# First group of a fused attention and FFN kernel: the leftover queries' product in front of the next k v

## The chip, the cores and the metric

One core of one Trainium2 chip. The metric is the device time of one execution in microseconds; the numbers below are medians of several runs. The engines are called PE (TensorE matmul; PEld are its weight loads), ACT (ScalarE), DVE (VectorE), POOL (GpSimd) and SP (SyncE, which issues most DMAs).

## What is computed

An attention block without softmax, its root-mean-square norm, and a feed-forward block with a product of two gates; all in float32:

```python
kv = np.einsum('bhsd,bhse->bhde', k, v)          # B, H, S, D = 8, 8, 576, 64
out = np.einsum('bhsd,bhde->bhse', q, kv)
rms = np.sqrt(np.mean(out * out, axis=-1, keepdims=True) + 1e-06)
x = (out / rms * g_norm)                          # to (B*S, H*D) = (4608, 512)
a = x @ w1                                        # 512 x 1024
b = x @ w2
h = a * b @ w3                                    # 1024 x 1024
return h @ w_out                                  # 1024 x 512
```

The kernel multiplies w3 by w_out first, and g_norm into w1 and w2.

## The kernel before

**Tiles and groups.** Each batch has 576 tokens. 512 of them form one group of the feed-forward part, and the 64 left over of all eight batches form a ninth group. So the loop at the end of the kernel runs over nine groups of 512 tokens. A group goes through four gate steps (p = 0 to 3, function `gates`, L896) and a projection (`project`, L1129, for group 0; `project_twice` for the others). Both use a Strassen-Winograd scheme (`winograd`, L724): seven products of half the size in each dimension, in place of eight. In the first group a gate product is 8 records of L738 in the profile (a float32 matmul leaves two records), a projection product 16. The seven products are p1 (a11 b11), p5 (s1 t1), u2 (s2 t2), then s4 b22, u3 (s3 t3), a12 b21 and a22 t4. Later groups apply the scheme twice and have other lines (L1030, L1288).

**Attention beside it.** While group T is multiplied, the attention of batch T + 1 is worked off in small pieces. `steps(b)` (L591) lists the pieces of batch b in eight steps, and `winograd` calls `between()` at two places, after u2 and in front of a22 t4; each call takes the next step. In group 0 the gate p = 0 takes none, so steps 0 and 1 stand in gate 1, 2 and 3 in gate 2, 4 and 5 in gate 3, and 6 in the projection after u2, 7 in front of its a22 t4. A step runs first its "ends" (what was begun in the step before and has to be finished), then its "fs".

**The pieces that matter.**
- `kv(g, beside)`, called by `begin_kv` (L497): k transposed times v for four heads, 36 matmuls of 64 x 64 (72 records of L350), then six small copies on ACT (L358, L360) into `kv_sb`. Its two result banks come from the pool `ps_at`, unless `beside` gives two banks: then it takes their last 64 columns. `begin_kv` afterwards has SP load the next k and v.
- `product(h)`, called by `finish(h)`: q times kv for half of the heads, 64 records of L428, into one bank of `ps_mm` and one of `ps_at` in batch 1; then `norm`.
- `product_left` (L438), for odd batches: the 64 leftover queries of this batch and of the one before, 32 records of L447, into two banks of `ps_at` (their first 256 columns). It reads `qT_left`, the transposed queries. For the odd batches 3 and 5 it has the k v of the next batch put into the same banks (L454, L455).
- `norm` (L388 on): squares on ACT (L395), sums on DVE (L396), a square root on ACT (L400), then reciprocal and multiplication on DVE (L402, L405). It is a generator with three parts; its first `next` issues squares and sums.
- Transposes through the DMA, `turn_by_dma`: a copy that puts the halves of the words apart (L309, L311), a transposing DMA on SP (L313), and a copy back (L323). In batch 1 the queries, `qT_left` and the first half of x have these copies on ACT, the second half of x and the leftover x on POOL. `qT_left` is begun in step 3 and finished among the ends of step 5, behind the ends of the first half of x in the list, and on ACT behind gate 3's copy u3.

**Order.** On PE, POOL and SP the instructions run in the order in which the program issues them. On ACT and DVE, in group 0, the compiler's planner orders them by readiness and by its own estimates of their cost; `tc.issue_after(x)` draws an edge that keeps instructions on x's engine behind x. A wait between two engines is put in wherever one uses the other's data.

**PSUM.** Eight banks: five in `ps_mm`, which the gate and projection products use, and three in `ps_at`, for attention.

Around the change, batch 1 before: step 5 issues the k v of batch 2 (first half), then the second q kv product of batch 1 with its norm. Step 6 issues the leftover product with its whole norm, and begins the transposes of the second half of x on POOL. Step 7 begins the transposes of the leftover x and of the next queries.

Of the kernel before, what the change touches and what calls it, by code (L numbers as in the profile page):

```python
# [22 lines left out]
def kernel(  # L23
# [36 lines left out]
    B, H, S, D = q.shape  # L60
# [4 lines left out]
    FIRST_OF_TWO = 2  # L65
# [18 lines left out]
    def bank(pool, tag):  # L84
        return pool.tile([P, 512], FP32, name=tag, tag=tag)

    loaded, copies, adds = {}, {}, {}
# [181 lines left out]
    def all_of(steps):  # L269
        for _ in steps:  # L270
            pass
# [61 lines left out]
    def attention(b):  # L333
# [55 lines left out]
        def norm(o_ps, dsts):  # L389

            n, w = len(o_ps), o_ps[0].shape[1]
            inv = work.tile([P, n, w // D], FP32, name="inv")
            for i in range(n):
                sq = work.tile([P, G], FP32, name=f"sq{0 if b > FIRST_OF_TWO else i}", bufs=1)[:, 0:w]
                nc.scalar.activation(sq, o_ps[i], AF.Square)  # L395
                adds["norm"] = nc.vector.tensor_reduce(  # L396
                    out=inv[:, i], in_=sq.rearrange("p (h d) -> p h d", d=D), axis=AX.X, op=ALU.add
                )
            yield
            nc.scalar.activation(inv, inv, AF.Sqrt, scale=1.0 / D, bias=eps_col)  # L400
            yield
            nc.vector.reciprocal(inv, inv)  # L402
            for i in range(n):
                m, k = dsts[i].shape[1:3]
                nc.vector.tensor_tensor(  # L405
                    out=dsts[i],
                    in0=o_ps[i].rearrange("p (m k d) -> p m k d", k=k, d=D),
                    in1=inv[:, i].rearrange("p (m k) -> p m k", k=k).unsqueeze(3).to_broadcast(
                        [P, m, k, D]
                    ),  # L410
                    op=ALU.mult,
                )
# [25 lines left out]
        def product_left():  # L438

            xn = st["left"] = work.tile([P, NP, 2, D], FP32, name="xn_left", bufs=1)  # L440

            o_ps = [bank(ps_at, "at") for _ in range(2)]
            for r in range(NP):
                for l in range(2):
                    for e in range(2):
                        rows = slice(e * D, (e + 1) * D)
                        nc.tensor.matmul(  # L447
                            o_ps[e][l * L:(l + 1) * L, r * D:(r + 1) * D],
                            lhsT=st["qT"][rows, r, l * L:(l + 1) * L],
                            rhs=kv_sb[(b - 1 + l) % 3][rows, r % 2 ^ e, e, r // 2, :],  # L450
                            start=True,
                            stop=True,
                        )
            if FIRST_OF_TWO < b < B - 1:  # L454
                batch(b + 1).begin_kv(0, o_ps)  # L455
            o_ps = [t[:, 0:NP * D] for t in o_ps]
            all_of(norm(o_ps, [xn[:, :, e:e + 1, :] for e in range(2)]))

        def turn(r):

# [58 lines left out]
        def finish(h):  # L519
            all_of(product(h))  # L520

        return SimpleNamespace(**{f.__name__: f for f in (
            start, begin_kv, begin_q, product, finish, turn, product_left,
            q_two_by_dma, q_by_dma, q_left_by_dma, x_by_dma, x_part_by_dma, x_left_by_dma, load_q_ahead,
        )})
# [3 lines left out]
    def batch(b):  # L529
        if b not in batches:  # L530
            batches[b] = attention(b)
        return batches[b]
# [58 lines left out]
    def steps(b):  # L591

        a = batch(b)
        a.start()
        more = b + 1 < B
        fs, ends = ([[] for _ in range(8)] for _ in range(2))

        def turn(i, f, *args, next_group=False):

            t = []

            def begin():
                t.append(f(*args))
                next(t[0])
                next(t[0])

            fs[i].append((begin,))  # L610
            (to_end if next_group else ends[i + 1]).append((lambda: all_of(t[0]),))

        if to_end:

            ends[0] += [(lambda: nc.gpsimd.tensor_copy(tick, late["p5"][:, 0, 0:1]),), *to_end]
        to_end.clear()
        odd = b % 2
        by_scalar, in_two = b >= FIRST_OF_TWO, b > FIRST_OF_TWO
        if b == 1:
            early.extend(a.q_two_by_dma(r) for r in (0, 1))  # L620
            q_first = list(early)
            fs[0].append((a.begin_kv, 0))

            def end_first():
                for t in q_first:
                    with tc.issue_after(copies["u3"][-1].ins):
                        next(t)
                    all_of(t)

            ends[1].append((end_first,))  # L630
        def begin_first():
            rest = a.product(0)
            next(rest)
            slots.setdefault(("p1", "p1"), []).insert(0, (all_of, rest))

        fs[2 if b == 1 else 1] += [
            (a.begin_kv, 1), (begin_first,) if by_scalar and not in_two else (a.finish, 0),
        ]
        if b == 1:
            last = {}  # L640

            def begin(name, behind, f, *args):
                last[name] = f(*args)
                with tc.issue_after(copies[behind][-1].ins):
                    next(last[name])
                next(last[name])

            def end(name, behind):
                with tc.issue_after(copies[behind][-1].ins):
                    next(last[name], None)  # L650
                all_of(last[name])

            fs[3] += [(begin, f"q{r}", "u3", a.q_two_by_dma, r) for r in (2, 3)]
            fs[3].append((begin, "left", "u3", a.q_left_by_dma))
            fs[4].append((begin, "x", "p1", a.x_by_dma, 0, nc.scalar.copy))
            ends[4] += [(end, "q2", "p1"), (end, "q3", "p5")]
            ends[5] += [(end, "x", "u2"), (end, "left", "u3")]
        elif by_scalar:
            turns_by_scalar(b)
        else:  # L660
            turn(1, a.q_two_by_dma, 2, 3)
            turn(2, a.x_by_dma, 0)
            if odd:
                turn(1, a.q_left_by_dma)
        second = 5 if b == 1 else 4
        if more:
            if not (in_two and odd):
                fs[second].append((batch(b + 1).begin_kv, 0))
        fs[second].append((a.finish, 1))
        if odd:  # L670
            fs[3 if in_two else second + 1].append((a.product_left,))
        if b == 1:
            turn(6, a.x_by_dma, 1)
            turn(7, a.x_left_by_dma, next_group=True)
        else:
            if not by_scalar:
                turn(5, a.x_by_dma, 1)
            if odd:
                turn(5, a.x_left_by_dma, next_group=more)
        if more and not by_scalar:  # L680
            turn(7 if b == 1 else 5, batch(b + 1).q_two_by_dma, 0, 1, next_group=True)
        if more:
            fs[7 if odd else 0].append((load_q_left, b + 1))
        return iter([lambda s=e + f: [f(*args) for f, *args in s] for e, f in zip(ends, fs)])
# [815 lines left out]

    for n, T in enumerate(groups):
        pieces = steps(T + 1) if n + 2 < NG else iter([])

        def prepare_some(pieces):
# [41 lines left out]
        for p in range(NF):  # L1546
# [22 lines left out]
            if T == 0:  # L1569
# [29 lines left out]
                if p + 1 == NF:  # L1599
                    allocate_projection()  # L1600
                    first, *others = zip(*(f(i) for i in range(NF) for f in (sum_ab, combine_w3o)))
                    with tc.issue_after(adds["c21"][p - 2].ins):
                        all_of(step() for step in first)
                    with tc.issue_after(adds["c12"][p - 1].ins):
                        all_of(step() for steps in others for step in steps)
# [57 lines left out]
```

## Time and profile before

| | |
|---|---|
| median of 3 runs | 743.08 us (742.86 to 744.15) |
| the profiled execution | 742.95 us, its span 741.0 us |
| granted clock of TensorE | 1.000 |
| PE idle from 82 us on, to the span's end | 3.4 us of 659.0 |
| small stretch of step 5 (k v, second q kv product) | 132.06 to 134.20 us |
| leftover product (step 6) | 146.49 to 147.11 us |

The span is the time from the first to the last instruction of one profiled execution. A timeline line gives start, duration, engine, line, operation, tiles, shape and count; what stands in brackets is the idle time before, with what ended it. Matmul durations overlap, since PE works on several at a time: distances between starts tell the pace. The chain of waits follows the work that ended last back from the end; where it names PE line after line, PE itself is what everything waits for. A record's "<-issue" means that the engine waited for nothing that the profile shows.

### The profile page before, as it was taken

The numbers are of one execution on the slowest core, as the hardware profiler recorded it, in microseconds if no ns is written. First come the engines' busy times: TensorE is split into PE (matmuls) and PEld (weight loads), VectorE is DVE, ScalarE is ACT, GpSimd is POOL, SyncE is SP. The second block draws the span as 40 slices with busy tenths as digits, with TensorE's granted clock in tenths as the row PEclk, the third lists the DMA queues.
The fourth block names the chain that finished last, engine by engine and source line by source line (L and its number), as shares of the span: only waits on it lengthen the run. The fifth ranks groups of instructions, "written<-read, shape, count | busy, mean of one in ns | idle before, by whom it ended". The sixth has DMA issues, their size and how long they took to land.

```text
span 741.0 us, 16817 instructions
## 1 busy us (share of the span) xinstructions
PE 735.2 (99%) x6839; PEld 658.3 (89%) x6839; DVE 622.0 (84%) x1237; ACT 379.0 (51%) x654; POOL 21.9 (3%) x29
## 2 busy tenths in 40 slices
PE   8999999999999999999999999999999999999998
PEld 6455788888899999999999999999999999999997
DVE  6877898967969689968996899689969987997797
ACT  6787777415552675257526752576177313212321
POOL 0000000131000000000000001000001000000000
PEclk9999999999999999999999999999999999999999
DMA  9997834599999698869986998588847762565454
GB/s 308 371 335 215 242 107 132 125 336 297 301 301 320 170 277 262 260 169 290 258 264 159 293 264 264 179 284 236 271 101 220 227 206 87 182 215 158 135 199 135
DMA packets 135456, 169.65 MB, mean 229 GB/s; under 512 B 78036, under 2 KB 110804, under 8 KB 135380
## 3 DMA queue, kind: packets, MB, share of 16 engines
q1 hardware_dynamic: 132928, 154.16, 69.0%
q10 hardware_dynamic: 2452, 14.42, 5.7%
q8 instruction: 54, 0.88, 0.5%
q14 instruction: 22, 0.18, 0.1%
HBM read 130.55 MB, written 20.71 MB: 204 GB/s over the span
## 4 chain that ended last, share of the span: by engine, by line
PE 97%; DMA 2%; ACT 0%; SPq 0%; issue 0%; DVE 0%; ACTq 0%
PE mm L738 38%; PE mm L1288 23%; PE mm L1030 21%; PE mm L708 7%; PE at L350 3%; PE at L738 2%; DMA raw<-in_moe_w_out_dram 2%; PE mm L428 1%; PE at L428 1%; PE at L695 1%; PE at L1331 0%; PE at L447 0%; PE at L370 0%; SPq L210 0%; ACT ab L162 0%; PE at L464 0%
## 5 line engine op out<-in xcount | busy, mean ns | idle before, releaser
L1079 ACT COPY slots<-mm 128x512 f32<-128x512 f32 x88 | 51.7, 587 | 126.3 <-PE mm L1288 83.3
L738 PE MATMUL mm<-xT,w_sb 128*128 128x256 f32 x448 | 102.9, 379 | 0.0
L738 PEld LDWEIGHTS mm<-xT,w_sb 128*128 128x128 f32 x448 | 84.4, 190 | 11.5 <-issue 0.5
L738 PE MATMUL mm<-xc,ws 128*128 128x256 f32 x336 | 76.1, 379 | 0.0
L738 PEld LDWEIGHTS mm<-xc,ws 128*128 128x128 f32 x336 | 63.8, 190 | 8.7
L756 ACT COPY slots<-mm 128x512 f32<-128x512 f32 x59 | 34.6, 587 | 68.9 <-PE mm L738 63.8
L708 PE MATMUL mm<-chunks,ab 128*128 128x512 f32 x128 | 60.7, 605 | 1.0 <-ACT chunks L163 0.8
L1083 DVE TENSOR_TENSOR slots<-mm,slots 128x512 f32<-128x512 f32 x66 | 45.1, 684 | 17.0 <-PE mm L1030 16.9
L1080 ACT COPY slots<-mm 128x384 f32<-128x384 f32 x88 | 42.4, 482 | 25.7 <-PE mm L1288 23.0
L1030 PE MATMUL mm<-ws,w3o_sb 128*128 128x128 f32 x350 | 53.9, 275 | 0.0
L396 DVE TENSOR_REDUCE inv<-sq 128x8 f32<-128x512 f32 (+1 forms) x40 | 24.6, 629 | 30.3 <-ACT sq L395 30.2
L1288 PE MATMUL mm<-w3o_sb,ab 128*128 128x128 f32 x368 | 48.9, 276 | 0.0
L1030 PEld LDWEIGHTS mm<-ws,w3o_sb 128*128 128x128 f32 x350 | 46.4, 192 | 0.0
L1288 PEld LDWEIGHTS mm<-w3o_sb,ab 128*128 128x128 f32 x368 | 45.4, 192 | 0.6
L1288 PE MATMUL mm<-w3o_sb,raw 128*128 128x128 f32 x340 | 43.5, 275 | 0.0
L708 PEld LDWEIGHTS mm<-chunks,ab 128*128 128x128 f32 x128 | 21.6, 190 | 23.4 <-issue 14.4
L1288 PEld LDWEIGHTS mm<-w3o_sb,raw 128*128 128x128 f32 x340 | 40.7, 192 | 0.0
L738 PE MATMUL mm<-xc,w_sb 128*128 128x256 f32 x160 | 38.5, 384 | 0.0
L1084 DVE TENSOR_TENSOR slots<-mm,slots 128x384 f32<-128x384 f32 x66 | 36.3, 551 | 2.3 <-PE mm L1288 1.9
L738 PE MATMUL mm<-xT,ws 128*128 128x256 f32 x160 | 38.1, 381 | 0.0
L323 ACT COPY xT<-xn 128x1024 uint16<-128x1024 uint16 x28 | 32.5, 1166 | 3.5 <-DMA xn<-xT 3.5
L738 PEld LDWEIGHTS mm<-xT,ws 128*128 128x128 f32 x160 | 30.1, 190 | 4.3 <-ACT slots L756 0.2
(243 smaller groups left out, 1639.8 us busy)
## 6 DMA issues: line engine op xcount, KB each, us to landing
w3o_sb<-w_l SPq DMA_DIRECT2D x21, 896.0 KB, 4.9
w3o_sb<-w3o_l SPq DMA_DIRECT2D x18, 896.0 KB, 6.6
raw<-in_moe_w_dram SPq DMA_DIRECT2D x31, 512.0 KB, 7.8
raw<-w3o_l SPq DMA_DIRECT2D x15, 896.0 KB, 4.7
w3o_sb<-w3o_l ACTq DMA_DIRECT2D x14, 896.0 KB, 4.5
k_sb<-in_k_dram SPq DMA_DIRECT2D x16, 576.0 KB, 4.9
v_sb<-in_v_dram SPq DMA_DIRECT2D x16, 576.0 KB, 6.4
q_sb<-in_q_dram SPq DMA_DIRECT2D x32, 256.0 KB, 3.9
```

The lines of the kernel that those rows point to most:

```text
L323: copy(words(dst), src)
L350: nc.tensor.matmul(ps[r * D:(r + 1) * D, :], lhsT=k_sb[rows, r, cols], rhs=v_sb[rows, r, cols], start=(j == 0), stop=(j == JS - 1),)
L396: adds["norm"] = nc.vector.tensor_reduce(out=inv[:, i], in_=sq.rearrange("p (h d) -> p h d", d=D), axis=AX.X, op=ALU.add)
L708: nc.tensor.matmul(sums_ps[half][m], lhsT=w3T[half, c][:, m, :], rhs=chunks[:, c, 1, :], start=(c == 0), stop=(c == KF - 1),)
L738: nc.tensor.matmul(ps[:, u, :], lhsT=lhsT(a_name, u, c), rhs=rhs(b_name, c),  start=(u == 0 and c == 0 and new), stop=(c == chunks - 1), s ...
L756: copies.setdefault(name, []).append(nc.scalar.copy(t, ps))
L1030: nc.tensor.matmul(ps[place // 4][:, place % 4, :], lhsT=x, rhs=y, start=new and place // 4 not in seen, stop=True, skip_group_check=True,)
L1079: nc.scalar.copy(z[:, 0:4], ps[0])
L1080: return nc.scalar.copy(z[:, 4:7], ps[1][:, 0:3])
L1083: nc.vector.tensor_add(z[:, 0:4], ps[0], z[:, 0:4])
L1084: nc.vector.tensor_add(z[:, 4:7], ps[1][:, 0:3], z[:, 4:7])
L1288: nc.tensor.matmul(ps[place // 4][:, place % 4, :], lhsT=x[:, c, :], rhs=y[:, c, :], start=new and place // 4 not in seen, stop=(c == 1), ...
```

## The change

For batch 1 only, three things. The leftover product is called in step 5 in place of the k v of batch 2, and has that k v put into its own two banks, right behind itself, as batches 3 and 5 do. The second q kv product follows, as before. The norm of the leftover product is no longer issued with it: `product_left` returns the generator, and step 6, where the leftover product was, runs the norm, with its first part behind the projection's copy u2 on ACT. The conditions for the other batches are written in another way and give the same calls.

```diff
-            if FIRST_OF_TWO < b < B - 1:
+            if b == 1 or FIRST_OF_TWO < b < B - 1:
                 batch(b + 1).begin_kv(0, o_ps)
             o_ps = [t[:, 0:NP * D] for t in o_ps]
-            all_of(norm(o_ps, [xn[:, :, e:e + 1, :] for e in range(2)]))
+            rest = norm(o_ps, [xn[:, :, e:e + 1, :] for e in range(2)])
+            if b > 1:
+                all_of(rest)
+            return rest
...
         second = 5 if b == 1 else 4
         if more:
-            if not (in_two and odd):
+            if not odd:
                 fs[second].append((batch(b + 1).begin_kv, 0))
+        if b == 1:
+            rest = []
+
+            def end_left():
+                with tc.issue_after(copies["u2"][-1].ins):
+                    next(rest[0])
+                all_of(rest[0])
+
+            fs[second].append((lambda: rest.append(a.product_left()),))
+            fs[second + 1].append((end_left,))
         fs[second].append((a.finish, 1))
-        if odd:
-            fs[3 if in_two else second + 1].append((a.product_left,))
+        if in_two and odd:
+            fs[3].append((a.product_left,))
```

## The prediction

> **What bounds the kernel now.** I read the page first, then the chain of waits, then the windows, then the timeline around the two places that the change touches. The page, its busy times and its chain by engine:
>
> ```profile
> PE 735.2 (99%) x6839; PEld 658.3 (89%) x6839; DVE 622.0 (84%) x1237; ACT 379.0 (51%) x654; POOL 21.9 (3%) x29
> ...
> PE 97%; DMA 2%; ACT 0%; SPq 0%; issue 0%; DVE 0%; ACTq 0%
> ```
>
> The windows view (stretch, length, then busy time and instructions of PE, PEld, DVE, ACT, POOL, then clock, DMA share, GB/s):
>
> ```profile
> 82.00:741.00 659.00, 655.64 (x6303) 614.40 (x6301) 558.44 (x1140) 317.44 (x561) 21.19 (x23) 1.00 0.73 219
> ```
>
> The reader is to see that TensorE sets the end, at full granted clock (1.00). From 82 us on, where the first group's gates begin, PE is idle for only 659.00 - 655.64 = 3.4 us, the tail after its last product included, and the wait table of PE has no entry at all in that stretch. So a stretch taken out of PE's row after 82 us comes off the end nearly in full, and no change here can win more than those 3.4 us by removing waits. What is left to win is time in which PE counts as busy but does not go at its best pace: at the switch between full 128x128 products and the small 64x64 ones.
>
> **The price of a switch.** The chain of waits gives stretches of PE with their lengths (start, us, what):
>
> ```profile
> 99.00 1.21 PE at L350 x72
> 100.21 12.29 PE mm L738 x56
> ...
> 146.56 0.62 PE at L447 x32
> 147.18 24.37 PE mm L738 x112
> ...
> 275.74 12.09 PE mm L738 x56
> ```
>
> 56 records of L738 that follow other full products take 12.09 us (last line), 0.2159 us each. The same 56 behind a k v take 12.29: 0.20 more. The 112 records behind the leftover product take 24.37, against 112 x 0.2159 = 24.18: 0.19 more. So every return from small to full products costs about 0.19 us, beside the small stretch itself. A leftover product that stands alone therefore costs 0.62 + 0.19 = 0.81 us of PE, as at 146.49:
>
> ```profile
> 143.80 2.75 PE L738 MATMUL mm<-raw 128*128 128x256 f32 x12
> 146.49 0.69 PE L447 MATMUL at<-kv_sb,qT_left 64*64 64x64 f32 x32
> 147.11 3.07 PE L738 MATMUL mm<-w3o_sb,raw 128*128 128x256 f32 x13
> ```
>
> Group 3 already has the order that the change gives the first group: leftover product, then k v in the same banks.
>
> ```profile
> 259.84 0.69 PE L447 MATMUL at<-kv_sb,qT_left 64*64 64x64 f32 x32
> 260.35 1.23 PE L350 MATMUL at<-v_sb,k_sb 64*64 64x64 f32 x72
> 261.51 0.71 PE L1030 MATMUL mm<-xc,w_sb 128*128 128x128 f32 x4
> ```
>
> From the first leftover matmul to the next full product it is 261.51 - 259.84 = 1.67 us. A k v alone is 1.21 (chain, first line above). So in front of a k v the leftover product adds 0.46 us, and its return to full products is paid already by the k v.
>
> **The change, part by part.**
>
> *PE, taken away* in the projection: 0.62 + 0.19 = 0.81. *PE, added* in gate 3: 0.46, because the stretch leftover, k v, second q kv product ends in the same return as now (at 134.20). Sum: -0.35 us. From the other side: if no return were saved and only the 1.21 + 0.62 - 1.67 = 0.16 between the starts counted, it would be -0.16. I take -0.35, since the two group-3 rows and the two return costs measure just this; -0.16 stays an end of the range.
>
> *A wait that is added.* The leftover product now stands first at 132.06 and reads qT_left, which ACT finishes just there:
>
> ```profile
> 130.44 0.59 ACT L756 COPY slots<-mm 128x512 f32<-128x512 f32 x1 [1.32 <-PE mm L738]
> 130.92 1.17 ACT L323 COPY qT_left<-ql_sb 128x1024 uint16<-128x1024 uint16 x1
> 134.41 2.23 ACT L323 COPY xT<-xn 128x1024 uint16<-128x1024 uint16 x2 [2.33 <-DMA xn<-xT]
> 136.56 0.20 ACT L358 COPY kv_sb<-at 128x64 f32<-128x64 f32 x1
> ```
>
> and the weight load that opens the small stretch today:
>
> ```profile
> 132.06 1.14 PEld L350 LDWEIGHTS at<-v_sb,k_sb 64*64 64x64 f32 x72 [0.33 <-issue]
> ```
>
> The copy ends at 130.92 + 1.17 = 132.09. How fast PE takes up an ACT copy the trace shows at 126.05 to 126.63: the weight load that waited for it begins at 126.68, 0.05 later. So the first leftover weight load can begin at 132.14 instead of 132.06: 0.08 us lost. Ends: nothing, if the copy is a little earlier; and 0.08 + 0.33 = 0.41, if the 0.33 that the weight loads stand idle at a switch (the line above) is only counted off after the wait. I take 0.08, since the small weight loads do not start before the full product is through anyway. Behind the waiting instruction on PE queue the k v, the second q kv product and gate 3's last product; nobody else waits for those closely: the k v's copies on ACT begin only at 136.56, behind the two xT copies.
>
> *PE in between.* From 132.14 to 147 everything on PE is 0.54 us later (0.46 + 0.08), then 0.27 earlier than now. The evictions and sums shift with it. What could be late: gate 3's c21, the projection's first products, the norm of product 1 (142.1) and the POOL copies behind it (142.17). The projection's combined x is first needed at 162.76 by L738 and its subtractions on DVE end at 159.5; the x copies on POOL end at 151.2 and DVE reads them at 154.39. Cover of 3 us each, so nothing. If that cover were gone, the loss would be at most the same 0.54.
>
> *SP, POOL, DMAs.* The k v's two loads (k and v of batch 2, second half) go out behind its reads, at 133.43 and 133.84 now, so some 0.5 later; they are first used at 171.48. The transposes of x on SP (144.54) and the POOL copies move by the same 0.5. No queue is passed by anything: the order on SP and POOL is as before. Price nothing.
>
> *PSUM.* The leftover product and the k v share two banks of ps_at, the second q kv product takes the third: three, as now. Two banks stay occupied until the leftover norm ends (149.13 + 0.76 = 149.9), and the next that asks for one is the k v at 171.48. Price nothing. The Trainium skill speaks against sharing here: "PSUM — Partial Sum Buffer", section "PSUM bank collisions raise a hardware error", says that two engines may not touch one bank in the same partitions at the same time, whatever the columns, so that such pairs get put one behind the other. By that rule ACT's k v copies and the leftover norm's readers would exclude each other; a k v copy lasts 0.2 to 0.43 us in this trace, so the rule would price a real clash at under 0.5. In the rows nothing clashes: the k v copies run from 136.56 to 137.85, the leftover's squares at 147.29.
>
> *The norm's end.* Its squares stay behind the projection's u2 copy (146.59) on ACT, by an explicit edge now. They no longer wait for PE. Its result is used by POOL at 151.17. Nothing.
>
> **Sum:** -0.35 + 0.08 = -0.27 us, between -0.35 + 0 = -0.35 and -0.16 + 0.41 = +0.25. The profiled execution took 742.95 (span 741.0 and 1.95 around it); with the change 742.68. The median of the three runs is 743.08, 0.13 above, so I forecast 743.08 - 0.27 = 742.8. That is 0.04%; under 0.2% (1.5 us) a measurement of this kernel can hardly tell a change from none.
>
> **Rivals.**
>
> 1. *The new wait eats the saving* (742.9 to 743.3). For it: copy and PE meet within 0.03 us, by chance. Against it: it can cost 0.41 at most, so it decides nothing at 0.2%. Chance 0.15.
>
> 2. *Slower: ACT's order.* In the call list the two xT copies stand ahead of qT_left's; only because their transposes land late (134.41) did the planner put qT_left first. If it puts them first now, qT_left's copy runs from 136.56 to 137.73 and PE stands from 132.06 to 137.78: 5.7 - 0.35 = +5.4, some 748.5. It decides from the point where even one xT copy comes first. Against it: all that is issued up to there is the same code, so the planner faces the same choice with the same costs. Chance 0.06.
>
> 3. *The planner sorts ACT and DVE anew further on*, since its estimated times for PE move by half a microsecond. Each product has its eviction due one product later (1.7 us in the gates, 3.5 in the projection), so a 2.2 us pair of copies put in front of one can cost PE 1 to 2 us, 744 to 745. A gain over 1.5 us would need half of PE's 3.4 us of idle time to vanish. Chance 0.09: slower by over 0.2% 0.04, within 0.02, faster 0.03.
>
> The forecast has 0.70. Faster by over 0.2%: 0.03. Within: 0.70 + 0.15 + 0.02 = 0.87. Slower: 0.06 + 0.04 = 0.10. For the range: the low end is 743.08 - 0.35, less the 0.22 by which the lowest run lies under the median, and 0.2 towards rival 3: 742.3. The high end is 743.08 + 0.25 and about half of the 1.07 by which the highest run lies above: 743.9.
>
> **What the next profile would show.** Right: one stretch at some 132.1, L447 x32, 72 of L350 starting 0.5 later, 64 of L428, and the full product back at some 134.75 (134.20 + 0.54); no L447 at 146.5 and no break in L738 there; qT_left's copy still at 130.92 with PE's first weight load within 0.1 of its end; the span 740.7. Wrong: a weight load of L447 marked as waiting for ACT for more than 0.4; qT_left's copy behind 134.41; a wait entry for PE after 82 us; a k v row in the first group that begins later than 0.5 after the leftover product.

## The result and the profile after

The changed kernel takes 744.7 us (median of 15 runs, 744.21 to 745.31), the kernel before 743.17 us in the same rounds (15 runs, 742.72 to 745.32): a ratio of 1.0017 [1.0010, 1.0024], so 1.5 us slower. The forecast was 742.8 us with a range up to 743.9: both the time and the sign are wrong. The profiled execution took 744.83 us, its span 742.7 (before 741.0). In the kernel after, the lines below the change stand 13 further down: L738 is now L751, L756 is L769.

First the page. Its busy times are those of before to within 1.5 us (PE 735.8 for 735.2, its weight loads 659.8 for 658.3) and its chain by engine is the same; nothing here tells where the loss is:

```profile
PE 735.8 (99%) x6839; PEld 659.8 (89%) x6839; DVE 621.7 (84%) x1237; ACT 378.7 (51%) x654; POOL 21.4 (3%) x29
...
q8 instruction: 54, 0.88, 0.5%
...
PE 97%; DMA 2%; ACT 0%; issue 0%; SPq 0%; DVE 0%; ACTq 0%
```

The wait table of PE from 82 to 741 us, empty before, has one entry (us in total, times, longest):

```profile
PE mm L428 <- issue: 1.6, 1, 1.6
```

This one stop is as large as the loss. The entry names no engine: "issue" means that PE waited for nothing that the profile ties to a semaphore. The chain of waits shows where it lies (start, us, what):

```profile
99.06 1.21 PE at L350 x72
100.27 12.28 PE mm L751 x56
...
132.19 0.70 PE at L447 x32
132.89 1.05 PE at L350 x72
...
134.52 1.64 issue
...
136.74 36.46 PE mm L751 x168
```

The chain of before at the same places, where the small stretch runs through and the first part of the projection ends at the leftover product (146.56, shown in the prediction):

```profile
132.13 1.21 PE at L350 x72
...
134.27 12.28 PE mm L738 x56
```

Two things are to be seen. The last line of the chain after the change is the projection without its break: 168 records in 36.46 us, where before they were 12.28 + 0.62 + 24.37 = 37.27 with the leftover product among them. The 0.81 us that the prediction took away is gone. And in the small stretch, which ran through before, PE stands for 1.64 us in the middle of the second q kv product, behind the 40th of its 64 records of L428. The timeline of PE there:

```profile
134.31 0.22 PE L428 MATMUL at<-kv_sb,qT 64*64 64x64 f32 x1
136.16 0.27 PE L428 MATMUL mm<-kv_sb,qT 64*64 64x64 f32 x1 [1.64 <-issue]
```

Records follow each other there at some 0.01 to 0.05 us; here 1.85 us lie between two starts. At the head of the stretch everything is as foretold. ACT's copy (first fence) and PE's first weight load (second fence):

```profile
130.98 1.17 ACT L323 COPY qT_left<-ql_sb 128x1024 uint16<-128x1024 uint16 x1
```

```profile
132.19 0.56 PEld L447 LDWEIGHTS at<-kv_sb,qT_left 64*64 64x64 f32 x32 [0.41 <-ACT qT_left L323]
```

The copy ends at 132.15, the weight load begins 0.04 later.

**The account.** The two spans cannot be compared directly, since the first k v starts at 99.00 us before and at 99.06 after. The spans, to the hundredth as the packed traces hold them, are 741.05 and 742.66. From that first k v to the end it is 741.05 - 99.00 = 642.05 us before and 742.66 - 99.06 = 643.60 after: +1.55. The parts: +1.85 for the stop, +0.07 for the wait (the stretch starts 0.13 later than before, of which 0.06 is that start), and the -0.35 of the prediction: +1.57.

### The profile page after: what moved, and what is told of

Read it like the earlier page. It is cut to its first block, busy times and chain, and to the rows that moved or that the text cites. A ratio compares the mean times of both kernels' runs of the same rounds, so it can differ in the third digit from the quotient of the medians.

```text
span 742.7 us, 16815 instructions
## 1 busy us (share of the span) xinstructions
PE 735.8 (99%) x6839; PEld 659.8 (89%) x6839; DVE 621.7 (84%) x1237; ACT 378.7 (51%) x654; POOL 21.4 (3%) x29
## 4 chain that ended last, share of the span: by engine, by line
PE 97%; DMA 2%; ACT 0%; issue 0%; SPq 0%; DVE 0%; ACTq 0%
PE mm L751 37%; PE mm L1301 23%; PE mm L1043 21%; PE mm L721 7%; PE at L350 3%; PE at L751 2%; DMA raw<-in_moe_w_out_dram 2%; PE mm L428 1%; PE at L428 1%; PE at L708 1%; PE at L1344 0%; PE at L447 0%; PE at L370 0%; SPq L210 0%; ACT ab L162 0%
## 5 line engine op out<-in xcount | busy, mean ns | idle before, releaser
L751 PE MATMUL mm<-xT,w_sb 128*128 128x256 f32 x448 | 102.9, 379 | 0.0
L751 PEld LDWEIGHTS mm<-xT,w_sb 128*128 128x128 f32 x448 | 84.5, 190 | 11.3 <-issue 0.5
L751 PE MATMUL mm<-xc,ws 128*128 128x256 f32 x336 | 76.1, 379 | 0.0
L751 PEld LDWEIGHTS mm<-xc,ws 128*128 128x128 f32 x336 | 64.0, 190 | 8.6
L769 ACT COPY slots<-mm 128x512 f32<-128x512 f32 x59 | 34.6, 586 | 68.2 <-PE mm L751 63.2
L751 PE MATMUL mm<-xc,w_sb 128*128 128x256 f32 x160 | 38.5, 384 | 0.0
L751 PE MATMUL mm<-xT,ws 128*128 128x256 f32 x160 | 38.1, 381 | 0.0
L751 PEld LDWEIGHTS mm<-xT,ws 128*128 128x128 f32 x160 | 30.1, 190 | 4.2 <-ACT slots L769 0.2
```

The lines of the kernel that those rows point to most:

```text
L751: nc.tensor.matmul(ps[:, u, :], lhsT=lhsT(a_name, u, c), rhs=rhs(b_name, c),  start=(u == 0 and c == 0 and new), stop=(c == chunks - 1), s ...
L769: copies.setdefault(name, []).append(nc.scalar.copy(t, ps))
```

## What the stop is: theories

**A, instruction supply.** PE's instructions come by a DMA queue of their own, the page's "q8 instruction": 54 packets, 0.88 MB, so 16 KB each. PE has 6839 matmul and 6839 weight-load records; (6839 + 6839) / 54 = 253, so a packet is a block of about 256 instructions of 64 bytes. Each small matmul of float32 leaves two matmul records and two weight loads. Among full products a block lasts 128 x 0.2159 = 28 us. The new stretch, with 32 + 72 + 64 = 168 matmul records and so 336 instructions in about 2.6 us, eats a block in 2 us. In the trace of before, the fetch of the block that is needed there starts before the stretch begins: the DMA view's queue table for 131 to 133 us of before (queue, kind, packets, MB, share) has it, and the packet itself, in the packed trace, starts at 131.42 and lands at 132.48.

```profile
q1 hardware_dynamic: 894, 0.22, 117.3%
q8 instruction: 1, 0.02, 3.3%
```

After, that window has no instruction packet; the one for 133 to 135 us has it, and nothing else moves there:

```profile
DMA packets 1, 0.02 MB, mean 8 GB/s; under 512 B 0, under 2 KB 0, under 8 KB 0
...
q8 instruction: 1, 0.02, 3.6%
```

The packet starts at 133.44, 2.0 us later than before, and lands at 134.60, when PE already stands; PE goes on at 136.16. The reading: PE's instruction reader runs ahead of the matmuls and asks for block n + 1 when it gets to block n. The wait for qT_left holds the reader at the head of the stretch, about 33 instructions short of the start of block n. Only when the copy lets go, at 132.15, can it ask (the packet starts 1.3 us later still, and no record shows why), and then PE eats the rest faster than the block comes: the stop stands 72 x 2 + 32 x 2 + 40 x 2 = 288 instructions into the stretch, and 288 = 32 + 256.

**B, data or bank.** The second product itself waits for something (kv_sb, qT, a bank of ps_at, the reads of the k v) that the profile doesn't name. Then the stop stays at its data wherever the blocks begin.

**C, density alone.** 336 small instructions in a row are too many for the supply whether or not something holds PE at their head. Then it stays also when the wait is gone.

## The experiments

Shifting the instruction count tells A from B. The start of the kernel has matmuls whose results aren't used (`keep_warm(n)`, n full products); putting a few of them against small ones moves every later instruction by a known number within its block and leaves the attention and the products as they are. The helper, in runs e1, e2, e4 and e12:

```python
def pad(n):
    t = bank(ps_mm, "mm")
    for i in range(n):
        cols = slice(i % 2 * D, (i % 2 + 1) * D)
        nc.tensor.matmul(t[cols, 0:D], lhsT=ident[0:D, 0:D], rhs=ident[0:D, 0:D], start=True, stop=True)
```

Each matmul is four instructions. The runs, with the span, the time from the first k v of group 0 to its end (the column that leaves out the scatter of the start), the start of the instruction packet, and PE's stop near 134 us. Spans and packet starts are read from the packed traces; all columns behind the median are of one profiled execution each:

| run | median us (runs) | span | first k v at | from there to the end | packet at | stop, us |
|---|---|---|---|---|---|---|
| before | 743.17 (15) | 741.05 | 99.00 | 642.05 | 131.42 | none |
| after | 744.7 (15) | 742.66 | 99.06 | 643.60 | 133.44 | 1.64, behind record 40 |
| e1_after_64 | 743.61 (12) | 741.08 | 99.32 | 641.76 | 127.96 | none |
| e2_before_64 | 743.26 (11) | 741.41 | 99.40 | 642.01 | 128.25 | none |
| e4_after_32 | 743.09 (1) | 740.95 | 99.15 | 641.80 | 129.82 | none |
| e12_after_16 | 744.68 (1) | 742.50 | 98.98 | 643.52 | 133.05 | 1.53, behind record 32 |
| e11_after_less32 | 745.51 (1) | 743.38 | 99.67 | 643.71 | 133.90 | 1.26, behind record 56 |
| e9_before_wait | 743.42 (1) | 741.48 | 99.08 | 642.40 | 133.19 | none named; PE 0.15 slower |
| e8_second_first | 742.26 (11) | 740.13 | 98.46 | 641.67 | 130.83 | none |
| e14_second_first_again | 742.59 (11) | 741.16 | 99.34 | 641.82 | 131.63 | none |
| e10_second_first_p5 | 742.51 (11) | 740.37 | 98.61 | 641.76 | 131.05 | none |
| e5_left_early | 743.93 (11) | 741.80 | 99.10 | 642.70 | 131.01 | none; 0.6 at 180 us |
| e13_left_early_p5 | 744.93 (11) | 742.42 | 99.06 | 643.36 | 131.03 | none; 1.4 at 186 us |
| e7_kv_first | 749.58 (4) | 747.48 | 98.58 | 648.90 | 130.88 | 4.0 for kv_sb |

### The block moved by 64: e1_after_64, e2_before_64

```diff
-        keep_warm(14)
+        keep_warm(12)
+        pad(18)
```

Both kernels, after and before, with 18 x 4 - 2 x 4 = 64 instructions more at the start.

> The changed kernel with 64 more PE instructions at the start (two of the 14 warm-up products replaced by 18 of 64x64), so that the small stretch at 132 us stands elsewhere in PE's blocks of 256 instructions (16384 B each in the instruction queue's packets). Theory A, instruction supply: PE's next block is asked for only when its sequencer passes a block's start; the wait for qT_left held the sequencer at the head of the stretch, 33 instructions short of such a start, so the block came 1.85 us late. With 64 more the start lies 31 instructions ahead of the wait: the gap in the second product (1.64 us in the changed kernel, behind the 40th of its 64 records) is gone, time 742.8, 0.3 under the kernel before. Theory B, a wait for data or a bank in the second product: place in the blocks does not matter, the gap stays at the same record, time 744.7. Theory C, density alone (336 small instructions in a row outrun the supply wherever they stand): a gap of 1 to 2 us stays at another record, time 744 to 744.7.

> The kernel before with the same 64 instructions more: what the padding itself costs. A, B and C: within 0.2 us of the kernel before (743.1), no gap in PE at 132 us; if the padding or a gap elsewhere cost anything, it would show here.

e1 takes 743.61 us, a ratio to before of 1.0005 [0.9997, 1.0014]; e2 743.26, 1.0000 [0.9991, 1.0008]. PE's wait table from 82 us on is empty in e1. Its weight loads' table still has the same wait at the head of the stretch (the pad's lines shift the numbers by 8):

```profile
PEld at L358 <- issue: 2.7, 8, 0.3
PEld at L455 <- ACT qT_left L331: 0.4, 1, 0.4
```

So the wait is there, the dense stretch is there, and the stop is gone: 64 instructions that have nothing to do with attention took it away. The chain of e1:

```profile
99.32 1.21 PE at L358 x72
...
132.47 0.69 PE at L455 x32
133.16 1.05 PE at L358 x72
...
135.14 36.46 PE mm L759 x168
```

From the k v at 99.32 to the end it is 641.76, 0.29 less than before: near the saving that the prediction foresaw (-0.27), without the stop. e1's span is 0.33 under that of e2, the same padding in both. The medians do not show this saving: e1's is 0.35 above e2's, and 0.8 above the 742.8 that I had expected. Five of e1's twelve runs lie at 744.07 to 744.76; the profiled one, at 743.21, is not among them, so what lengthened them is open. In the profiled executions the first k v comes 0.3 later than before (99.32, and 99.40 in e2), though e14 below has 99.34 without any padding, so what the padding costs at the start isn't settled.

### Smaller shifts: e4_after_32, e12_after_16, e11_after_less32

The same edit with `keep_warm(13)` and `pad(9)` (32 instructions more), `keep_warm(13)` and `pad(5)` (16 more), and `keep_warm(6)` without a pad (32 fewer).

> The changed kernel with 32 more PE instructions at the start (one of the warm-up products replaced by 9 of 64x64). A: the block's start now lies 1 instruction behind the head of the stretch, so the sequencer still meets it only after the wait; the block after it is used up 32 instructions earlier: the gap stays at 1.5 to 1.9 us and moves to the 24th of the 64 records of the second product (40th in the changed kernel). B: the gap stays at the 40th. Span 742.7 to 743.0.

> The changed kernel with 16 PE instructions more at the start: how far ahead of the held instruction PE still asks for a block. With the start 33 instructions ahead it did not (changed kernel), with 1 it did. A: either the request at 133.4 and a gap of 1.85 us at the 32nd record, or the request at 130 to 131 and no gap; nothing in between.

> The changed kernel with 32 PE instructions fewer at the start (6 warm-up products in place of 14). A: the block's start lies 65 instructions behind the head of the stretch, out of reach of the held sequencer, and the block is used up 32 instructions later than in the changed kernel, still inside the stretch: the gap is there, 1.4 to 1.9 us, and moves to the 56th of the 64 records of the second product. If 64 more instructions took the gap away for another reason than their place in the blocks (the 18 small products, say), then it stays at the 40th record.

If the stop is the end of a block, 16 instructions more must bring it 8 matmul records forward, from the 40th to the 32nd, and 32 fewer must put it 16 back, to the 56th. It is so. The timeline of e12, the 33rd record (its second product is L436):

```profile
135.87 0.27 PE L436 MATMUL mm<-kv_sb,qT 64*64 64x64 f32 x1 [1.53 <-issue]
```

and of e11, the 57th:

```profile
136.62 0.27 PE L428 MATMUL mm<-kv_sb,qT 64*64 64x64 f32 x1 [1.26 <-issue]
```

The same data, the same banks, another record: B falls. From the packet's start to PE's going on it is 136.16 - 133.44 = 2.72 us after, 135.87 - 133.05 = 2.82 in e12 and 136.62 - 133.90 = 2.72 in e11. What PE still had to run after the packet's start, 2.72 - 1.64 = 1.08 us after, 1.29 in e12 and 1.46 in e11, is what makes the stops differ. Their places came as expected; their sizes, 1.53 and 1.26, are under the 1.85 and the 1.4 to 1.9 that I had named.

e4 missed its expectation: I had foreseen a stop behind the 24th record, and there is none. With 32 more, block n begins at the head of the stretch itself, and its packet starts at 129.82, before the wait: so the reader reaches at least that far ahead while it is held. In e12 block n begins some 17 instructions behind the head and its packet comes late. How far ahead a held reader reaches therefore lies between about 1 and 17 instructions here; I didn't narrow it further.

e11 had a second, smaller stop that I had not foreseen: PE's wait table of e11 has two lines,

```profile
PE mm L428 <- issue: 1.3, 1, 1.3
PE at L428 <- issue: 0.3, 1, 0.3
```

the second at 490 us in another group's q kv product:

```profile
490.66 0.27 PE L428 MATMUL at<-kv_sb,qT 64*64 64x64 f32 x1 [0.31 <-issue]
```

The packed trace of e11 has 7424 records of PE between the two points at which it goes on: matmuls, weight loads and 66 semaphore and drain instructions. That is 29 x 256, to the record, and the two late packets, at 133.90 and 488.41, are 29 packets apart. So the second stop is the end of a block too, and the block's length of 256 is measured here and no longer only worked out from an average. Moving the count can thus also bring a stop where there was none.

### The wait alone: e9_before_wait

The kernel before, with one small matmul that reads qT_left in front of the k v; its result isn't used.

```diff
...
+            if b == 1:
+                fs[second].append((a.touch_left,))
             if not (in_two and odd):
                 fs[second].append((batch(b + 1).begin_kv, 0))
```

Here `touch_left` is the added matmul, 64 x 64.

> The kernel before with one more 64x64 product of qT_left in front of the k v (its result is not used): the wait alone, without the leftover product. A: the sequencer is held to 132.14, the block is asked for at about 133.4 as in the changed kernel, and the stretch of 276 instructions ends 13 short of the block's end: the gap comes later, in gate 3's last product, and is 0.2 to 0.8 us, since those 13 instructions take some 1.4 us; span 741.3 to 741.9. B: a wait of 0.1 us at the new product and nothing else, span 741.1. C: nothing, span 741.1.

The wait alone, without the leftover product in the stretch, makes the packet late: it starts at 133.19 (before 131.42), where A had said 133.4. The stretch is then short by the leftover product's instructions, so the stock ends only among the first full products behind it: eight records of gate 3's last product take 1.98 us there in place of 1.83. From the first k v to the end it is 642.40, 0.35 more than before, of which 0.19 is the stretch with its added matmul and 0.15 these records. The expectation of 0.2 to 0.8 for the stop was a little too high. What this one run shows: the wait is what delays the request; how much of the delay reaches PE depends on how fast the following instructions are eaten.

### No wait at the head: e8_second_first, e14_second_first_again, e10_second_first_p5

The second q kv product first, then the leftover product and the k v. The stretch is as dense as in the kernel after, but its first 128 instructions wait for nothing, and qT_left is done 1.1 us before the leftover product comes (131.54 and 132.68).

```diff
+            fs[second].append((a.finish, 1))
             fs[second].append((lambda: rest.append(a.product_left()),))
             fs[second + 1].append((end_left,))
-        fs[second].append((a.finish, 1))
+        else:
+            fs[second].append((a.finish, 1))
```

> The changed kernel with the second q kv product first, then the leftover product and the k v: the wait for qT_left stands 128 instructions into the stretch, behind the block's start. A: the block is asked for at about 131.4, no gap at 134, no wait for qT_left, one return to full products saved: PE 0.35 under the kernel before, 742.75, unless ACT's copy at 180 us, which has 0.8 us to spare in the kernel before, is late again. B and C: a gap of 1 to 2 us, 744.5.

742.26 us, 0.9987 [0.9978, 0.9996] of before. The packet starts at 130.83, and the chain shows the stretch whole:

```profile
98.46 1.21 PE at L350 x72
...
132.68 0.47 PE at L447 x32
133.14 1.05 PE at L350 x72
134.19 36.46 PE mm L753 x168
170.65 1.21 PE at L350 x72
```

C falls: 168 small records in a row are supplied, if nothing holds PE in front of them. From the first k v to the end it is 641.67: 0.38 less than before, near the -0.35 of the prediction's PE sum.

The median gains 0.8, though, more than twice that. The first k v comes at 98.46 here and at 99.00 before, 0.5 earlier, in a stretch that the edit doesn't touch. The same kernel again:

> The kernel with the second product first once more. It measured 742.26, 0.8 under the kernel before, of which its profile puts 0.36 behind the k v at 99 us and 0.54 in front of it (98.46 in place of 99.00), where no edit lies and where the weights' first loads from HBM set the pace. If the early part is chance of the load, the time is 742.7 this time; if it belongs to the program (where its data lie, say), 742.3 again.

742.59 against 743.11, 0.9992 [0.9983, 1.0001], its span 741.2, its first k v at 99.34. From there to the end it is 641.82, 0.23 less than before, where e8 had 0.38 less: two executions of one kernel differ by 0.15 in this column, so a closer agreement with -0.35 would be chance. And 98.46 was no work of the edit: the start scatters; e8's second load of w_out landed at 15.20 us, that of before at 15.72. Why the runs of e8 as a whole gained 0.8 and those of e14 0.5 stays partly open. The order beats the kernel after by over 2 us in both, and the kernel before by 0.5 to 0.8, the second time with an interval that just touches 1.

e10 adds another edit to e8: in group 1 the norm of the first product stands behind the copy p5 in place of p1.

> As the kernel with the second product first, and in group 1 the norm of its first q kv product goes on (square root on ACT and what follows) behind gate 1's copy p5 in place of its copy p1, so that this copy no longer queues behind a square root that waits for DVE. If the new wait at 180 us, seen with qT_left finished early (1.0 us for a copy of L769), is that queue's, it cannot come: 742.7, with fewer runs above 743.8. If not, as the kernel with the second product first.

742.51 us, 0.9991 [0.9982, 1.0000], 641.76 from the first k v on: no gain over e8.

### The copy earlier: e5_left_early, e13_left_early_p5

The other way to take the wait away: qT_left's copy back behind gate 3's u2 in place of u3.

```diff
-            ends[4] += [(end, "q2", "p1"), (end, "q3", "p5")]
-            ends[5] += [(end, "x", "u2"), (end, "left", "u3")]
+            ends[4] += [(end, "q2", "p1"), (end, "q3", "p5"), (end, "left", "u2")]
+            ends[5] += [(end, "x", "u2")]
```

> The changed kernel with qT_left finished one step earlier, behind gate 3's copy u2 (127.6 us) in place of u3, so that PE does not wait for it at 132 us; the PE instructions and their places in the blocks are those of the changed kernel. A: the sequencer runs ahead again, the block is asked for at about 131.4 as in the kernel before (133.44 in the changed one), no gap, and the 0.08 us of waiting go too: 742.75. B: the gap stays, 744.6. C: the gap stays, 744.6.

743.93 us, 1.0012 [1.0003, 1.0020]. The packet starts at 131.01, no stop at 134, no wait for qT_left: again A. But the gain is lost elsewhere, at 180 us in group 1, where e5's timeline of PE has

```profile
181.10 1.99 PE L751 MATMUL mm<-xT,ws 128*128 128x256 f32 x8 [0.56 <-ACT slots L769]
```

PE waits for a bank that ACT empties late. On ACT a square root (L400) that waits for DVE's sums stands in front of that copy:

```profile
177.17 0.58 ACT L769 COPY inner_sums<-mm 128x512 f32<-128x512 f32 x1 [1.40 <-PE mm L751]
179.32 0.31 ACT L400 ACTIVATE inv<-inv,eps_col 128x16 f32<-128x16 f32 x1 [1.57 <-DVE inv L396]
179.54 1.03 ACT L311 COPY qT<-q_sb 128x1024 uint16<-128x1024 uint16 x1
180.47 0.58 ACT L769 COPY slots<-mm 128x512 f32<-128x512 f32 x1
```

I took the square root's place for the cause and moved the norm behind the copy p5:

> The kernel with qT_left finished early (gap at 134 gone, but PE waits 1.0 us at 180 for a copy of L769 behind ACT's square root), with that square root moved behind gate 1's copy p5. If the square root's wait for DVE is what made the copy late, the wait at 180 goes: from the k v at 99 us to the end 641.7 (642.0 in the kernel before, 642.7 with qT_left early), time 742.8. If the copy is late for another reason: 742.7 from there, time 743.9.

744.93 us, 1.0022 [1.0013, 1.0031]: slower still. The wait at 180 went, so the square root did hold that copy; but a larger wait came, 1.4 us at 186, behind an ACT copy that waits for DVE's xn. The square root's place is thus not what costs the time. What stays is that DVE itself is late: with the copy of qT_left moved, the xT copy behind it on ACT (L309) begins 1.10 later (129.22 for 128.12 in the kernel after), SP's transposes of x begin at 145.30 (143.79 in the kernel after), the stores behind them on SP follow, and DVE's additions at L1191, which wait for one of these stores, begin at 166.48 and 171.91. Counted from the first k v, that is 1.6 and 1.9 later than in e8 (164.24 and 169.39, L1193 there) and 1.2 later than in the kernel before (165.19 and 170.66, L1178). That chain is read from the traces; it was not tried by itself.

### The k v first: e7_kv_first

The k v in front of the leftover product, in the same two banks.

```diff
             o_ps = [bank(ps_at, "at") for _ in range(2)]
+            if b == 1:
+                batch(b + 1).begin_kv(0, o_ps)
...
-            if b == 1 or FIRST_OF_TWO < b < B - 1:
+            if FIRST_OF_TWO < b < B - 1:
                 batch(b + 1).begin_kv(0, o_ps)
```

> The changed kernel with the k v first and the leftover product behind it, in the same two banks: the wait for qT_left stands 144 instructions into the stretch, behind the block's start. A: the block is asked for early, no gap, 742.8. B, if the second product waits for the readers of the shared banks: the gap stays, 744.7. C: the gap stays, 744.7.

The packet starts at 130.88 and there is no stop for it, as A says, but the expectation missed a wait of another kind: 749.58 us, 1.0085 [1.0072, 1.0099]. PE's wait table has

```profile
PE at L449 <- ACT kv_sb L360: 4.0, 2, 3.8
```

and ACT's timeline says why:

```profile
130.50 1.17 ACT L323 COPY qT_left<-ql_sb 128x1024 uint16<-128x1024 uint16 x1
133.86 2.23 ACT L323 COPY xT<-xn 128x1024 uint16<-128x1024 uint16 x2 [2.19 <-DMA xn<-xT]
135.99 0.20 ACT L358 COPY kv_sb<-at 128x64 f32<-128x64 f32 x1
136.21 0.42 ACT L360 COPY kv_sb<-at 64x64 f32<-64x64 f32 x2
```

The leftover product writes into a bank that ACT has yet to read, and ACT reads it only behind the two xT copies, which wait for their transposes until 133.86. In the kernel after, with the k v written last, nothing is written behind ACT's reads. The prediction cited the Trainium skill, "PSUM — Partial Sum Buffer", section "PSUM bank collisions raise a hardware error", for such a pair being put one behind the other whatever the columns; here PE's writes and ACT's reads are in different columns of one bank, and PE does wait. The page gives no time for it, and the run's 4.0 us is the queue on ACT, not the 0.2 to 0.4 us of a copy.

## Why the prediction was wrong

- *PE, taken away and added, -0.35*: right. The projection lost the 0.81 us; e8 and e14 show the sum at -0.38 and -0.23, e1 at -0.29 with the wait's 0.07 in it. The stretch, less the stop, is 136.67 - 132.19 - 1.85 = 2.63 us long; foretold were 134.75 - 132.14 = 2.61.
- *A wait that is added, 0.08, with ends at nothing and 0.41*: this is the step that failed. As a wait for data it cost 0.07, and its place (copy's end, weight load 0.04 later) is as foretold. But the step named what is queued behind the waiting instruction as work alone, "the k v, the second q kv product and gate 3's last product", and found that "nobody else waits for those closely". What was also held there is PE's reading of its own instructions, and with it the request for the next block: its packet started at 133.44, against 131.42 before and 131.01 in e5, which has the same instructions without the wait. That cost 1.85 us, over four times the upper end. The page had the queue ("q8 instruction", 54 packets), but the prediction has no term for it and does not set 336 instructions in 2.6 us beside a block of 256.
- *PE in between; SP, POOL, DMAs; PSUM; the norm's end*: nothing, and nothing was lost there. The k v's loads went out 0.6 later (134.03 for 133.43), as said. SP's transposes did not move by 0.5 to the late side, they came at 143.79 in place of 144.54; it cost nothing either way.
- *Rivals*: rival 1, the new wait, had the right place with a price of 0.41 at most. Rival 2 did not come: qT_left's copy was first on ACT. Of rival 3 nothing showed; the order of ACT's 654 instructions is that of before, and on DVE only a few of the 1237 changed places, at 153 to 158 us, with no wait of PE behind them.
- *The signs*: "a wait entry for PE after 82 us" was named as one that would make the prediction wrong, and that is what came. By the letter a second sign came too, a k v row later than 0.5 behind the leftover product (132.71 - 132.19 = 0.52); it tells nothing, since group 3 of the kernel before has 0.51. The span foretold was 740.7, it is 742.7: 2.0 apart, of which 1.85 is the stop, 0.06 the start of the first k v; 0.1 stays.
- *The range* took its upper end, 743.9, from the 0.41 for the wait and half of the scatter of the runs before. The 0.41 is the gap to the copy's end and the idle time of the weight loads at a switch: neither bounds what a held engine costs.

On the supply, the Trainium skill, "Runtime: NRT & Kernel Launch", section "Instruction fetch mechanics", says that instructions are refilled in 16 KiB blocks of 256 and that crossing into the next is mostly hidden. The trace agrees on the block (packets of 16 KB, 7424 = 29 x 256 records between e11's stops), and in the kernel before on the hiding; the kernel after has one crossing that is not hidden, of 1.64 us.

What was not tried: a stretch with fewer instructions and the same wait at its head, the reach of a held reader between 1 and 17 instructions, and a wait put further up among the full products. What the reader does is worked out from the packets' starts; no record shows the reader itself.

## What to carry to other kernels

A wait in front of a dense run of small matmuls is to be priced twice: by how long the engine stands, and by the instruction block whose request stands with it. Count the instructions behind the wait (here four for each small float32 matmul): if they come near a block of 256 and run as fast as here (336 in 2.6 us), put a run of instructions that waits for nothing at the head, as e8 does with 128, and the wait behind it. An "issue" entry like these (0.3 to 1.6 us) in the middle of like instructions is read against the packets of the instruction queue before data or banks are suspected, and a few padding instructions at the kernel's start tell the two apart.

## What the runs showed of the hardware

- TensorE's instructions came in packets of 16,384 bytes; the median packet was 0.96 us on its way in the kernel before and 0.98 in the kernel after, the three late ones 1.16 to 1.26. PE went on 2.7 to 2.8 us after the late packet's start (after, e12, e11), which is 1.5 to 1.6 us after its landing; no record explains that part.
- With a wait at the head of the stretch, the packet came early when a block starts at the waiting instruction (129.82 in e4), and late when it starts about 17 further (133.05 in e12), one run each.
- So the time of a kernel can move by 1.8 us with 32 instructions at its start: from the first k v to the end 641.80 us with 32 more, 643.60 without and 643.71 with 32 fewer.
